# Set-up fills off GpSimd, a new order of the first transfers, a longer hold-back and three-operand VectorE forms in a three-layer kernel

## The chip, the core and the metric

One core of a Trainium2 chip runs the whole program. The metric is the device time of one execution in microseconds (us), taken as the median of several runs. One of the executions is recorded by the hardware profiler, and all rows below come from that one.

## The reference

Three layers follow each other, on 4 x 576 = 2304 tokens of width 512:

```python
scores = (q @ k.T) / 8                 # 8 heads of 64, each row sees the 64 positions up to itself
attn = exp(scores - max) / (sum + 1e-9)
x = attn @ v                           # (2304, 512)
x = relu(x @ w_in) ** 2 @ w_out        # 512 -> 2048 -> 512
do = x @ w_skip > 0                    # tokens that go to an expert, about half
e = argmax(x @ w_gate); p = softmax(x @ w_gate)[e]
out = x;  out[do] += p * (relu(x[do] @ w1[e]) @ w2[e])   # 8 experts, 512 -> 1024 -> 512
```

The weights w_in and w_out are handed over as 64-bit floats, and products are made in split precision: a value is a rounded part and a remainder, and three products stand for one.

## The kernel before

**Chunks and units.** The 18 token tiles of 128 form nine chunks of two. A unit (c, j) of the dense layer is one eighth of its hidden width for one chunk: `l1` makes 24 products of 256 columns, ScalarE squares the result and rounds it to `gh`, VectorE makes the remainder `gl` (line 491), and `l2` makes 24 products of 512 columns into two accumulators, one for each token tile. `l2` runs two units behind `l1`. The pool `gp` keeps `gh` and `gl` in three buffers.

**The first stage.** Before the units run, ten steps (`for s in range(10)`) issue the attention of tiles 0 to 3 in eight groups of four heads: scores and a mask on TensorE (`at_qk`), a maximum (L288), a scaling of it by 1/8 (L291), four exponentials on ScalarE (L302), the sum's guard and reciprocal (L306, L308), the division (L309), a transpose (`at_tr`, L317 and L319) and the product with v (`at_pv`, L335, L343, L344). Between them weights are converted from 64-bit floats (`conv_next`): ScalarE scales the high words (L220), GpSimd clips them (L221), VectorE builds the 32-bit value in three instructions (L223, L225, L227), ScalarE rounds it (L233), GpSimd makes the remainder (L234). All the loads lie on SyncE's queue, in the order in which they are issued.

**Set-up.** `setup_masks` builds the attention masks on GpSimd; `setup_routing`, called after step 4, fills the constants of the routing with GpSimd memsets and writes a table of 144 KB to memory. When tile t has its scores, `load_next` fetches q and k of the next tile with the same buffer. From tile 6 on q is padded with zeros: `load_qk(6)` first clears the buffer with two GpSimd memsets (L160, L161).

**The scheduler.** Outside of blocks marked `manual_schedule` a list scheduler orders each engine's instructions by its own estimate of time, with the program's order as priority; inside of them TensorE keeps the written order.

**The end of the dense layer.** Of the last chunk the `l2` of the last `TAIL` = 3 units is held back: first tile 0 of each (so that its routing may start), then tile 1 of each, as cover for the routing of tile 0.

**The experts.** Each expert has one block of 128 tokens that always runs (`static`) and more that run if there are that many (`extras`). `ex_x` transposes the gathered tokens on TensorE; ScalarE rounds the transposed tokens, VectorE takes the remainder (`ex_split`), and 24 products with w1 follow (`l1e`, L831). Gathers and scatters are indirect transfers from GpSimd's queue. Their descriptors live in a scratch of 8192 bytes per partition.

Of the kernel before, what the change touches and what calls it, by code (L numbers as in the profile page):

```python
# [8 lines left out]
F32 = mybir.dt.float32  # L9
F32R = mybir.dt.float32r  # L10
# [4 lines left out]
ALU = mybir.AluOpType  # L15
# [4 lines left out]
P = 128  # L20
# [15 lines left out]
HOMES = (1, 2, 0, 1, 2, 1)  # L36
# [11 lines left out]
DOT00 = 6  # L48
ROW = NE * NT
FILLS = ((2, 3), (1, 2), (1, 0), (2, 3), (2, 0), (0, 5))  # L50
TAIL = 3
FE = 1024
KF = FE // P
WIN = 64
FAR = 1 << 20
# [7 lines left out]
def body(ctx, tc, qt_d, kt_d, vw_d, wi_d, wo_d, w9_d, w9r_d, w1_d, w2_d, out):  # L63
    nc = tc.nc
# [9 lines left out]
    small = pool("small", 4)  # L74
    xtp = pool("xtp", 2)
    rp = pool("rp", 2)
    gp = pool("gp", 3)
    dram = pool("dram", 1, space=DRAM)
    ps_h = pool("ps_h", 2, space=PSUM)
    ps_acc = pool("ps_acc", 1, space=PSUM)  # L80
# [11 lines left out]
    def psa():  # L92
        turn[0] += 1
        return ps_a[turn[0] // 2 % len(ps_a)].tile([P, 512], F32, tag="a", name="a")

    def sm():
        return sp.tile([P, 512], F32, tag="sm", name="sm")
# [35 lines left out]
            out=mask.rearrange("p a b -> p (a b)"), in_=maskb.rearrange("p a b -> p (a b)"))  # L133

    def setup_routing():
        nc.gpsimd.memset(ones, 1.0)
        nc.gpsimd.memset(tri, 1.0)
        nc.gpsimd.affine_select(
            out=tri, in_=tri, pattern=[[1, P]], compare_op=ALU.is_gt,
            fill=0.0, base=0, channel_multiplier=-1)  # L140
        nc.gpsimd.iota(io8i, pattern=[[1, NE]], base=0, channel_multiplier=0)
        nc.gpsimd.tensor_copy(out=io8, in_=io8i)
        nc.gpsimd.iota(route[:, :, 0], pattern=[[P, NT]], base=0, channel_multiplier=1)
        nc.gpsimd.memset(ohsum[:, 0, :], 0.0)
        fill = sm().bitcast(I32)
        nc.gpsimd.memset(fill, FAR)
        nc.scalar.dma_start(
            out=tab_v.rearrange("p r c -> p (r c)"), in_=fill[:, 0:2 * ROW])
        nc.scalar.dma_start(out=w9, in_=w9_d)
# [6 lines left out]
    def load_qk(t):  # L156
        i = home(t)
        k_ = kvs[i > 0].tile([P, NPAIR, P + WIN], F32, tag=f"k{i}", name="k")
        if t == len(HOMES):
            nc.gpsimd.memset(qpad[0:64, :, 1, :], 0.0)  # L160
            nc.gpsimd.memset(qpad[64:128, :, 0, :], 0.0)  # L161
        if t < len(HOMES):
            nc.sync.dma_start(
                out=q_s[i], in_=qt_d[t].rearrange("h d a b -> (h d) a b"))
        else:
            for h in range(2):
                nc.sync.dma_start(out=qpad[64 * h:64 * h + 64, :, h, :], in_=qt_d[t, h])
        nc.sync.dma_start(out=k_, in_=kt_d[t])
        kt_t[t] = k_

    def load_v(t):
        i = home(t)
        v_ = kvs[i > 0].tile([P, 2, DM], F32, tag=f"v{i}", name="v")
        nc.sync.dma_start(out=v_, in_=vw_d[t])
        vw_t[t] = v_

    def load_next(t, load):
        later = [n for n in range(t + 1, NT) if home(n) == home(t)]
        if later:
            load(later[0])  # L180
# [75 lines left out]
    def at_qk(t, g):  # L256
        s = bank("qk", t, g)
        i, k_ = home(t), kt_t[t]
        early = t // CT in EARLY
        if early:  # L260
            nc.tensor.matmul(
                s.rearrange("p (a b) -> p a b", a=2), lhsT=identb,
                rhs=mask_of(t, maskb).unsqueeze(1).to_broadcast([P, 2, 2 * P]),
                start=True, stop=False, skip_group_check=True)
        for pi in range(2):
            for blk in range(2):
                u = 2 * pi + blk
                pr = 2 * g + pi
                cols = slice(u * P, (u + 1) * P)
                if t >= len(HOMES):  # L270
                    nc.tensor.matmul(
                        s[:, cols], lhsT=qpad[:, 2 * pr + blk].rearrange("p a b -> p (a b)"),
                        rhs=k_[:, pr, 64 * blk:64 * blk + P],
                        start=not early, stop=True, skip_group_check=early)
                    continue
                for h in range(2):
                    half = slice(64 * h, 64 * h + 64)
                    nc.tensor.matmul(
                        s[half, cols], lhsT=q_s[i][half, 2 * pr + blk],
                        rhs=k_[half, pr, 64 * blk:64 * blk + P],  # L280
                        start=not early, stop=True, skip_group_check=early)
        if g == 1:
            load_next(t, load_qk)
        ef = sm()
        e = ef.rearrange("p (a b) -> p a b", a=4)
        nmx = small.tile([P, 4], F32, tag="nmx", name="nmx")
        if early:
            nc.vector.tensor_reduce(  # L288
                out=nmx, in_=s.rearrange("p (a b) -> p a b", a=4), axis=AX.X, op=ALU.max,
                negate=True)  # L290
            nc.vector.tensor_scalar(  # L291
                out=nmx, in0=nmx, scalar1=1.0 / 8.0, scalar2=None, op0=ALU.mult)
        else:
            mk = mask_of(t, mask)
            for u in range(4):
                nc.vector.tensor_tensor_reduce(  # L296
                    out=e[:, u, :], in0=s[:, u * P:(u + 1) * P],
                    in1=mk[:, u % 2 * P:(u % 2 + 1) * P], scale=-1.0 / 8.0, scalar=HUGE,
                    op0=ALU.add, op1=ALU.min, accum_out=nmx[:, u:u + 1])
        sums = small.tile([P, 4], F32, tag="sum", name="sum")  # L300
        for u in range(4):
            nc.scalar.activation(  # L302
                out=e[:, u, :], in_=s[:, u * P:(u + 1) * P] if early else e[:, u, :],
                func=AF.Exp, bias=nmx[:, u:u + 1],
                scale=1.0 / 8.0 if early else -1.0, accum_out=sums[:, u:u + 1])
        nc.vector.tensor_scalar(  # L306
            out=sums, in0=sums, scalar1=1e-9, scalar2=None, op0=ALU.add)
        nc.vector.reciprocal(out=sums, in_=sums)  # L308
        nc.vector.tensor_tensor(  # L309
            out=e, in0=e, in1=sums.unsqueeze(2).to_broadcast([P, 4, P]), op=ALU.mult)  # L310
        p_t[t, g] = e

    def at_tr(t, g):
# [154 lines left out]
    def l1(c, j):  # L468
        early = bool(raw_q)
        hp = h_early[0] if early else ps_h.tile([P, 512], F32, tag="h", name="h")  # L470
        hp = hp.rearrange("p (a b) -> p a b", a=2)
        r = rp.tile([P, 512], F32, tag="r", name="r")
        xt = xt_t[c]
        for f in range(2):
            for k in range(KD):
                o = (k % 2) * 256 + f * P
                mm3(hp[:, f, :], wi_t[j, k // 2][:, 0, o:o + P], wi_t[j, k // 2][:, 1, o:o + P],
                    xt[:, 0, k, :], xt[:, 1, k, :], k == 0, k == KD - 1)
            if early:
                nc.scalar.activation(  # L480
                    out=r[:, f * CTOK:(f + 1) * CTOK], in_=hp[:, f, :], func=AF.Relu)
        if not early:
            nc.scalar.activation(  # L483
                out=r, in_=hp.rearrange("p a b -> p (a b)"), func=AF.Relu)
        gh = gp.tile([P, 2, CTOK], F32R, tag="gh", name="gh")
        gl = gp.tile([P, 2, CTOK], F32R, tag="gl", name="gl")
        ghf = gh.rearrange("p a b -> p (a b)")
        glf = gl.rearrange("p a b -> p (a b)")
        nc.scalar.activation(out=r, in_=r, func=AF.Square)  # L489
        nc.scalar.copy(out=ghf, in_=r)  # L490
        nc.vector.tensor_tensor(out=glf, in0=r, in1=ghf.bitcast(F32), op=ALU.subtract)  # L491
        g_t[c, j] = (gh, gl)

    def l2(c, j, tiles=range(CT), parts=range(2)):
# [104 lines left out]
    if True:  # L599
# [8 lines left out]
        load_qk(0)  # L608
        conv_load()
        load_qk(1)  # L610
        load_v(0)
        conv_load()
        load_qk(2)
        load_v(1)
        conv_load()
        load_v(2)
        conv_load()
        for _ in range(LOOK - 4):
            conv_load()
        setup_masks()  # L620
        acc_pool[1] = ps_s
        qk, tr, pv = grp_ops(0)
        qk1, tr1, pv1 = grp_ops(1)
# [3 lines left out]
        for s in range(10):  # L627
            if s < 8:
                qk[s]()
            if 1 <= s < 9:  # L630
                tr[s - 1]()
            if 2 <= s:
                pv[s - 2]()
            for _ in range(PRO[s]):
                conv_next()
            if s == 4:
                setup_routing()

        def w_free(kind, j):
            slot_q.extend((wp, w_tag[kind, j, h]) for h in range(2))  # L640
# [172 lines left out]

        def ex_x(tx, inner=True):
            xg = tx[2]
            pp = psa()
            for k in range(KD):
                nc.tensor.transpose(pp[:, k * P:(k + 1) * P], xg[:, k * P:(k + 1) * P], ident)
            return ex_split(pp, inner)

        def ex_block(e, tx, xt, fill=lambda i: None, nxt=lambda: None, late=False):
            ti, gw, xg, _ = tx
# [176 lines left out]
```

## Time and profile before

| what | before |
|---|---|
| median of 3 runs (lowest, highest) | 686.37 us (684.65, 687.01) |
| the profiled execution | 685.27 us, of which its span is 683.6 us |
| mean granted TensorE clock | 0.989 |
| busy TensorE, VectorE, ScalarE, GpSimd | 656.6, 415.3, 357.5, 155.4 us |

The page gives each engine's busy time, the span in 40 slices and the costliest groups. A view by windows gives the busy time of each engine in chosen stretches. The timeline gives instructions in order of time: start and duration in us, engine, line, operation, tiles written and read, count, and in brackets the idle time of the engine before it with what ended it. The profiled execution lies 1.1 us under the median.

### The profile page before, as it was taken

The page shows a single profiled execution, that of the slowest core. Times are in us where ns is not written, and L with a number is a line of the kernel's source. Part 1 is how long each engine was busy: PE and PEld are TensorE (multiplying, and loading weights), DVE is VectorE, ACT ScalarE, POOL GpSimd, SP SyncE. Part 2 cuts the span into 40 slices and gives each one's busy share as a digit, 9 for nine tenths or more (in the row PEclk, how much of TensorE's full clock was granted, in tenths as well). Part 3 has the DMA queues.
Part 4 walks back from the last instruction along what each step waited for, and adds up shares of the span by engine and source line. Part 5 has one row for each costly group of instructions (what it writes and reads, how often), then busy time and mean ns, then how long its engine had stood idle before and what let it go on. Part 6 is the DMA issues. An engine that isn't in the chain of part 4 may idle for free. (4 is left out here: it accounts for less than half of the span.)

```text
span 683.6 us, 12514 instructions
## 1 busy us (share of the span) xinstructions
PE 656.6 (96%) x4569; PEld 566.7 (83%) x4569; DVE 415.3 (61%) x1200; ACT 357.5 (52%) x821; POOL 155.4 (23%) x185
## 2 busy tenths in 40 slices
PE   7799999999999999999999999999999999999995
PEld 4588888989899889898989989899988777777774
DVE  4999977449627727716725824942735644288981
ACT  4887756544535444635535444544641544277761
POOL 5557666100100100000000000030001513044641
PEclk9899999999999999999999999999999999999998
DMA  8965453053203203203112121206592347559500
GB/s 332 349 206 172 147 168 111 1 203 98 70 32 102 70 32 101 70 32 102 40 61 85 48 71 50 83 26 230 177 317 100 111 151 279 224 161 337 222 12 8
DMA packets 45605, 88.72 MB, mean 130 GB/s; under 512 B 17806, under 2 KB 18062, under 8 KB 45392
## 3 DMA queue, kind: packets, MB, share of 16 engines
q1 hardware_dynamic: 42112, 83.38, 35.6%
q0 software_dynamic: 2976, 3.95, 1.8%
q8 instruction: 47, 0.77, 0.5%
q10 hardware_dynamic: 432, 0.32, 0.2%
q14 instruction: 38, 0.31, 0.1%
HBM read 79.07 MB, written 12.49 MB: 134 GB/s over the span
## 5 line engine op out<-in xcount | busy, mean ns | idle before, releaser
L464 PE MATMUL h<-xt,wi 128*128 128x256 f32 x576 | 165.3, 287 | 2.1 <-ACT r L480 2.1
L465 PE MATMUL h<-xt,wi 128*128 128x256 f32 x576 | 165.6, 287 | 0.3 <-DVE xt L344 0.3
L466 PE MATMUL h<-xt,wi 128*128 128x256 f32 x576 | 164.0, 285 | 0.0
L464 PE MATMUL acc<-wo,gh 128*128 128x512 f32 x288 | 116.3, 406 | 1.1 <-ACT gh L490 1.0
L464 PEld LDWEIGHTS h<-xt,wi 128*128 128x128 f32 x576 | 110.6, 192 | 6.4 <-ACT r L480 3.1
L465 PEld LDWEIGHTS h<-xt,wi 128*128 128x128 f32 x576 | 110.6, 192 | 3.4 <-DVE xt L344 0.6
L465 PE MATMUL acc<-wo,gh 128*128 128x512 f32 x288 | 112.6, 393 | 0.0
L466 PE MATMUL acc<-wo,gl 128*128 128x512 f32 x288 | 112.0, 393 | 0.0
L491 DVE TENSOR_TENSOR gl<-r,gh 128x512 fp32r<-128x512 f32 x72 | 52.4, 728 | 96.5 <-ACT gh L490 95.0
L466 PEld LDWEIGHTS h<-xt,wi 128*128 128x128 f32 x576 | 110.7, 192 | 0.0
L456 POOL DMA_INDIRECT tab_d<-route,posi x18 | 19.5, 1084 | 362.6 <-DVE posi L447 263.7
L483 ACT ACTIVATE r<-h 128x512 f32<-128x512 f32 x58 | 34.5, 595 | 98.4 <-PE h L466 94.7
L375 DVE CUSTOM_DVE_ANT_0 prod<-sm,w9b 128x512 f32<-128x512 f32 x108 | 74.0, 685 | 1.9 <-ACT sm L352 1.5
L466 PEld LDWEIGHTS acc<-wo,gl 128*128 128x128 f32 x288 | 54.1, 188 | 12.6 <-DVE gl L491 0.8
L464 PEld LDWEIGHTS acc<-wo,gh 128*128 128x128 f32 x288 | 54.1, 189 | 11.1 <-ACT gh L490 2.1
L465 PEld LDWEIGHTS acc<-wo,gh 128*128 128x128 f32 x288 | 54.3, 189 | 8.6 <-issue 0.2
L548 DVE TENSOR_TENSOR e_s<-e_s,e_s 128x1024 fp32r<-128x1024 f32 x34 | 42.1, 1258 | 11.9 <-ACT e_s L546 11.5
L302 ACT ACTIVATE sm<-sm,nmx 128x128 f32<-128x128 f32 x96 | 37.5, 392 | 20.7 <-DVE nmx L296 20.3
L319 ACT COPY sm<-a 128x512 f32<-128x512 f32 x36 | 21.4, 594 | 48.8 <-PE a L317 48.8
L489 ACT ACTIVATE r<-r 128x512 f32<-128x512 f32 x72 | 45.6, 634 | 1.5
L490 ACT CAST gh<-r 128x512 fp32r<-128x512 f32 x72 | 44.6, 619 | 1.5
L546 ACT CAST e_s<-e_s 128x1024 fp32r<-128x1024 f32 x42 | 42.9, 1050 | 2.5 <-PE acc L466 2.0
(205 smaller groups left out, 1144.6 us busy)
## 6 DMA issues: line engine op xcount, KB each, us to landing
e_s<-in_w_dram SPq DMA_DIRECT2D x54, 512.0 KB, 6.4
v<-in_vw_dram SPq DMA_DIRECT2D x18, 512.0 KB, 3.4
ri<-in_wi_dram SPq DMA_DIRECT2D x16, 512.0 KB, 4.1
ro<-in_wo_dram SPq DMA_DIRECT2D x16, 512.0 KB, 3.7
k<-in_kt_dram SPq DMA_DIRECT2D x18, 384.0 KB, 4.2
e_r<-in_w_dram SPq DMA_DIRECT2D x10, 512.0 KB, 6.6
x_d<-sm SPq DMA_DIRECT2D x17, 256.0 KB, 2.5
out_dram<-sm SPq DMA_DIRECT2D x17, 256.0 KB, 3.1
```

Of the source, the lines that this page charges most:

```text
L302: nc.scalar.activation(out=e[:, u, :], in_=s[:, u * P:(u + 1) * P] if early else e[:, u, :], func=AF.Exp, bias=nmx[:, u:u + 1], scale=1.0 ...
L319: nc.scalar.copy(out=pt, in_=pp)
L375: nc.vector.tensor_tensor_reduce(out=prod, in0=x2_t[t], in1=w9b_t[0][:, j, :], scale=1.0, scalar=0.0, op0=ALU.mult, op1=ALU.add, accum_out ...
L464: nc.tensor.matmul(out_ap, lhsT=ah, rhs=bh, start=start, stop=False)
L465: nc.tensor.matmul(out_ap, lhsT=ah, rhs=bl, start=False, stop=False)
L466: nc.tensor.matmul(out_ap, lhsT=al, rhs=bh, start=False, stop=stop)
L483: nc.scalar.activation(out=r, in_=hp.rearrange("p a b -> p (a b)"), func=AF.Relu)
L489: nc.scalar.activation(out=r, in_=r, func=AF.Square)
L490: nc.scalar.copy(out=ghf, in_=r)
L491: nc.vector.tensor_tensor(out=glf, in0=r, in1=ghf.bitcast(F32), op=ALU.subtract)
L546: nc.scalar.copy(out=hi, in_=raw)
L548: eng.tensor_tensor(out=lo, in0=raw, in1=hi.bitcast(F32), op=ALU.subtract)
```

## The change

It does seven things. The memsets of `setup_routing` go to VectorE, and the call moves up to just behind `setup_masks`. The first loads get another order: each weight load but the first and last comes one load of v earlier. q and k of tile 6 are loaded after the scores of tile 5 instead of those of tile 2, with the two memsets that precede them. Four VectorE instructions (L291, L306, L309, L491) are written in the form that has two tensors and a scalar; two of them get a tile of zeros as second tensor. `TAIL` becomes 4 and `gp` gets a fourth buffer. For the blocks of `extras`, `ex_x` works in two halves in two PSUM banks. The scratch of the indirect transfers is halved.

```diff
-TAIL = 3
+TAIL = 4
-    gp = pool("gp", 3)
+    gp = pool("gp", 4)
     def setup_routing():
-        nc.gpsimd.memset(ones, 1.0)
-        nc.gpsimd.memset(tri, 1.0)
+        nc.vector.memset(ones, 1.0)
+        nc.vector.memset(tri, 1.0)
...
-        nc.gpsimd.memset(ohsum[:, 0, :], 0.0)
+        nc.vector.memset(ohsum[:, 0, :], 0.0)
         fill = sm().bitcast(I32)
-        nc.gpsimd.memset(fill, FAR)
+        nc.vector.memset(fill, FAR)
...
-        if g == 1:
+        if g == 1 and t != 2:
             load_next(t, load_qk)
+        if g == 1 and t == len(HOMES) - 1:
+            load_next(2, load_qk)
...
-            nc.vector.tensor_scalar(
-                out=nmx, in0=nmx, scalar1=1.0 / 8.0, scalar2=None, op0=ALU.mult)
+            nc.vector.scalar_tensor_tensor(
+                out=nmx, in0=nmx, scalar=1.0 / 8.0, in1=tiny.to_broadcast([P, 4]),
+                op0=ALU.mult, op1=ALU.add)
...
-        nc.vector.tensor_scalar(
-            out=sums, in0=sums, scalar1=1e-9, scalar2=None, op0=ALU.add)
+        nc.vector.scalar_tensor_tensor(
+            out=sums, in0=sums, scalar=1e-9, in1=tiny.to_broadcast([P, 4]),
+            op0=ALU.add, op1=ALU.add)
         nc.vector.reciprocal(out=sums, in_=sums)
-        nc.vector.tensor_tensor(
-            out=e, in0=e, in1=sums.unsqueeze(2).to_broadcast([P, 4, P]), op=ALU.mult)
+        nc.vector.scalar_tensor_tensor(
+            out=e, in0=e, scalar=1.0, in1=sums.unsqueeze(2).to_broadcast([P, 4, P]),
+            op0=ALU.mult, op1=ALU.mult)
...
-        nc.vector.tensor_tensor(out=glf, in0=r, in1=ghf.bitcast(F32), op=ALU.subtract)
+        nc.vector.scalar_tensor_tensor(
+            out=glf, in0=r, scalar=1.0, in1=ghf.bitcast(F32), op0=ALU.mult, op1=ALU.subtract)
...
         load_qk(1)
+        conv_load()
         load_v(0)
+        load_qk(2)
         conv_load()
-        load_qk(2)
         load_v(1)
         conv_load()
         load_v(2)
-        conv_load()
         for _ in range(LOOK - 4):
             conv_load()
         setup_masks()
+        setup_routing()
...
-            if s == 4:
-                setup_routing()
...
+        def ex_x_halves(xg):
+            hi = gp.tile([P, 512], F32R, tag="gh", name="xh2")
+            lo = gp.tile([P, 512], F32R, tag="gl", name="xl2")
+            pps = [psa(), psa()]
+            cut = [slice(n * 256, (n + 1) * 256) for n in range(2)]
+            for n in range(2):
+                for k in range(2):
+                    nc.tensor.transpose(
+                        pps[n][:, k * P:(k + 1) * P],
+                        xg[:, (2 * n + k) * P:(2 * n + k + 1) * P], ident)
+                nc.scalar.copy(out=hi[:, cut[n]], in_=pps[n][:, 0:256])
+            for n in range(2):
+                nc.vector.tensor_tensor(
+                    out=lo[:, cut[n]], in0=pps[n][:, 0:256], in1=hi[:, cut[n]].bitcast(F32),
+                    op=ALU.subtract)
+            return hi, lo
...
-                   dynamic_dma_scratch_size=8192)
+                   dynamic_dma_scratch_size=4096)
```

## Rows read from the trace of the kernel before

**Rows 1.** The page, its first part: TensorE's busy time, share, instructions.

```profile
PE 656.6 (96%) x4569; PEld 566.7 (83%) x4569; DVE 415.3 (61%) x1200; ACT 357.5 (52%) x821; POOL 155.4 (23%) x185
```

**Rows 2.** By windows: us, PE, PEld, DVE, ACT, POOL busy; clock, DMA share, GB/s.

```profile
24.00:28.00 4.00, 2.70 (x49) 2.13 (x50) 3.97 (x5) 3.06 (x14) 3.16 (x6) 1.00 1.12 284
...
32.00:36.00 4.00, 3.73 (x28) 3.35 (x27) 4.00 (x11) 2.89 (x11) 1.77 (x3) 0.50 0.91 295
```

**Rows 3.** Timeline of ScalarE, first stage: the first three weight scalings.

```profile
7.18 0.67 ACT L220 ACTIVATE ri<-ri 128x512 f32<-128x512 f32 x1 [4.44 <-DMA ri<-in_wi_dram]
...
11.32 0.69 ACT L220 ACTIVATE ri<-ri 128x512 f32<-128x512 f32 x1 [0.94 <-DMA ri<-in_wi_dram]
...
15.53 0.68 ACT L220 ACTIVATE ri<-ri 128x512 f32<-128x512 f32 x1 [1.63 <-DMA ri<-in_wi_dram]
```

**Rows 4.** Timelines of VectorE, GpSimd, ScalarE and TensorE from 24 to 31 us.

```profile
24.34 2.90 DVE L291 TENSOR_SCALAR nmx<-nmx 128x4 f32<-128x4 f32 x1
...
24.32 0.52 POOL L160 MEMSET qpad<- 64x512 f32 x1
24.81 1.27 POOL L234 TENSOR_TENSOR wi<-f,wi 128x512 fp32r<-128x512 f32 x1
...
26.06 0.52 POOL L146 MEMSET sm<- 128x512 int32 x1
26.56 0.66 POOL L221 TENSOR_SCALAR ro<-ro 128x512 f32<-128x512 f32 x1
...
27.34 0.37 ACT L302 ACTIVATE sm<-s,nmx 128x128 f32<-128x128 f32 x1 [0.94 <-DVE nmx L291]
...
28.89 0.38 PE L261 MATMUL s<-maskb,identb 128*128 128x512 bf16 x1 [1.47 <-ACT sm L302]
...
30.71 1.11 PE L317 MATMUL a<-ident,sm 128*128 128x128 f32 x4 [0.43 <-DVE sm L309]
```

**Rows 5.** Timeline of TensorE: one product of `l1` at either clock.

```profile
33.33 0.41 PE L466 MATMUL h<-xt,wi 128*128 128x256 f32 x1
...
38.08 0.28 PE L465 MATMUL h<-xt,wi 128*128 128x256 f32 x1
```

**Rows 6.** By line (durations min/median/max in ns); timelines of GpSimd and VectorE.

```profile
L291 DVE TENSOR_SCALAR nmx<-nmx x12: 155/417/2899, 8.6 to 76.5; 128x4 f32<-128x4 f32 x12
...
L309 DVE TENSOR_TENSOR sm<-sm,sum x36: 676/690/1798, 11.9 to 450.6; 128x512 f32<-128x512 f32 x36
...
59.76 1.30 POOL L234 TENSOR_TENSOR wi<-f,wi 128x512 fp32r<-128x512 f32 x1 [1.59 <-ACT wi L233]
...
60.39 1.21 DVE L309 TENSOR_TENSOR sm<-sm,sum 128x512 f32<-128x512 f32 x1
```

**Rows 7.** By line: the padded scores, with their first and last start.

```profile
L271 PE MATMUL a<-k,qpad x192: 270/275/275, 140.2 to 446.6; 128*128 128x128 f32 x192
```

**Rows 8.** Timelines of ScalarE and TensorE at the end of the dense layer.

```profile
510.46 1.04 ACT L546 CAST e_s<-e_s 128x1024 fp32r<-128x1024 f32 x1
...
513.01 0.62 ACT L490 CAST gh<-r 128x512 fp32r<-128x512 f32 x1
...
513.68 0.50 PE L464 MATMUL acc<-wo,gh 128*128 128x512 f32 x1 [1.00 <-ACT gh L490]
```

**Rows 9.** TensorE's waits (total, times, longest); timelines of an extra block; a half cast.

```profile
PE h L831 <- ACT xh L729: 2.2, 3, 0.7
...
570.10 0.63 PE L818 MATMUL a<-ident,sm 128*128 128x128 f32 x4 [0.95 <-DVEq L900]
570.81 0.59 ACT L729 CAST xh<-a 128x512 fp32r<-128x512 f32 x1 [2.65 <-PE a L818]
...
28.72 0.38 ACT L343 CAST xt<-xp 128x256 fp32r<-128x256 f32 x1
```

**Rows 10.** Indirect gathers: duration by line; issues with median us to landing.

```profile
L705 POOL DMA_INDIRECT xg<-x_d,tabs x15: 1012/1293/2043, 534.9 to 647.3; - x15
...
xg<-x_d,tabs POOLq DMA_INDIRECT x15, 3.5
```

More of the change, by code (lines that the diff above doesn't have):

```diff
@@ L815, in ex_x @@
             xg = tx[2]
+            if inner:
+                return ex_x_halves(xg)
             pp = psa()
```

## The prediction

> **What bounds the kernel now.** The first part of the page comes first: TensorE is busy for 96% of the span [rows 1], so only time in which it waits, or in which its clock is low, can be won. The view by windows says where that is. Two stretches of the first stage stand out [rows 2]: from 24 to 28 us TensorE is busy for 2.70 of 4.00 us while VectorE is full with five instructions, and from 32 to 36 us TensorE is nearly full, but its granted clock is 0.50. From the end of that stage to the end of the dense layer TensorE runs without gaps worth naming, so whatever the first stage gives back is kept until the end. The reader then looks at TensorE's waits and the timelines around them: a wait of 1.00 us at the end of the dense layer [rows 8] and three waits of some 0.7 us in front of extra blocks [rows 9]. The other engines matter only where they end one of these.
>
> **The order of the first transfers.** ScalarE waits for the second and third weight loads, 0.94 and 1.63 us [rows 3], and its queue is in order, so the exponentials behind them wait too. The landings that released the first and the second scaling lie 4.14 us apart, and between them the queue carried 1664 KB (v of tile 0, one weight load, q and k), so 512 KB take 1.27 us. In the new order the second and third weight loads lie 512 KB further ahead: the first wait goes, the second shrinks by 1.27. Against that, the table of 144 KB that `setup_routing` writes now goes out at the start, 0.36 us at the same rate. v comes 1.27 us later; its first use lies after all of this. I take 1.0 us; the ends are 0.3 (other work of ScalarE fills the time) and 1.3.
>
> **The stall of VectorE.** L291 scales a tile of 4 columns, and at 24.34 it takes 2.90 us [rows 4]. All that time GpSimd runs without a gap: the clearing of the padded q (L160), a remainder (L234), the fill of the table (L146) and a clip (L221), and L291 ends as the last one does. The change takes the memsets out of the place: the fill goes to VectorE, at the start, where VectorE has nothing to do, and the clearing goes behind tile 5. The price on TensorE's path is not 2.75 us, though: ScalarE had other work and waited for 0.94, then TensorE for 1.47 before the next scores and 0.43 before the next transpose [rows 4]. Without the stall the scores start 0.94 us earlier and the transpose another 0.4: I take 1.4 us. The ends are 0.9 and 2.7, the whole of it, since VectorE is full until 36 us and all its later work comes earlier.
>
> **The clock.** After that low stretch the granted clock is 0.50 from 32 to 36 us [rows 2], the lower of the two levels, and a product of `l1` takes 0.41 us against 0.28 [rows 5]. At the same pace these 4 us hold 2 us of work, and with their edges some 3 us could be won at full clock. If TensorE waits less before, the clock need not fall. But then TensorE catches up with VectorE, which is full in that stretch. I take 1.5 us; the ends are 0 and 3.
>
> **The three-operand forms.** What they do where GpSimd is at work is in no row. For the two large ones the nearest row is the form they replace: L309 at 60.39 has both inputs in SBUF and takes 1.21 us instead of 0.68 at the least; it ends 0.54 us after L234, which started before it [rows 6]. I take it that the new form, with the same two inputs, waits likewise: nothing gained, nothing lost; at most what all the small stalls hold. L291 has a median of 0.42 us against 0.16 at the least [rows 6], so its twelve lose some 0.26 us each beside the long one, 3 us in all up to 77 us, of which I count a third in the first stage: an end of 1 us. The Trainium skill speaks here against part of the change (SBUF — State Buffer, section "Who interferes with whom"): a `tensor_scalar` in its two-port mode is blocked by any GpSimd instruction, while an instruction with two SBUF inputs is blocked by one that reads SBUF. By that rule L309 and L491 gain nothing and L291 is freed from memsets alone; the trace agrees on the two old forms (1.21 us beside L234, 2.90 us across memsets too). If the new form were free of GpSimd, the sum would be about 1 us larger.
>
> **Tile 6.** Its q and k are loaded later, with two memsets of 0.52 us (1.04 us of GpSimd, which waits for ScalarE most of the time), and SyncE's queue holds the weight loads behind them for as long, which are five ahead. By the code they are issued at least three units before their first use at 140.2 us [rows 7]. Nothing.
>
> **The hold-back.** At 513.68 TensorE has waited 1.00 us for `gh` of the last unit [rows 8]: ScalarE put casts of expert weights (L546) of 1.04 us each, two of them, ahead of its own steps. With `TAIL` = 4 the last `l1` comes half a unit earlier, and tile 0 of one more unit stands in front of the product that waits: six products of 512 columns more between the two, over 1 us even by the 0.28 us of one of 256 columns [rows 5]. The wait goes, 1.0 us; the wait for `gl` behind it may give 0.15. The second of those casts then goes into a buffer that is freed only by the held-back unit, so it can't stand in front any more. The loads of two w2 parts of expert 2 move behind the routing of the last tile, and are used only in expert 1's block. Ends 0 (ScalarE finds other work to put in front) and 1.2. Work is moved, not added.
>
> **The halves.** In front of an extra block TensorE makes four transposes (0.63 us), ScalarE casts 512 columns (0.59), and the first product waits for 0.7 [rows 9]. With halves the cast starts after two transposes, 0.3 us earlier, and takes 0.38, the row of a cast of 256 columns, so the first product comes 0.3 + 0.2 = 0.5 us earlier; the second cast is ready before the third product asks for it. There are three such waits; at the first ScalarE is still with the cast before, so only 0.2 there. Together 1.2, less some for two more instructions per block: I take 1.0, with ends 0.4 and 1.3.
>
> **The sum.** 1.0 + 1.4 + 1.5 + 1.0 + 1.0 = 5.9 us. The profiled execution took 685.27 us and would take 679.4; it lies 1.1 us under the median, and against the median it is 686.37 - 5.9 = 680.5 us. A fourth buffer of `gp` costs nothing but room; the halved scratch is costed at nothing, with a rival of its own.
>
> **The rivals.** (a) The clock falls again in the first stage, in the same place or another. For it: the clock also depends on gaps that stay. It takes back the 1.5: 682.0 us. (b) The first stage refills: ScalarE and VectorE are close to full there, the scheduler orders them anew, and the change hardly does there what it says. Then the first stage gives 1.0 of its 3.9 us: 683.4. (c) The new form isn't held up by GpSimd at all, and VectorE, the engine that is full in the first stage, gets the small stalls back too, with the whole 2.7 of the long one and the clock: 3 us more, about 677.5. Against it stands the row of the old form with two inputs. (d) Slower: the halved scratch holds too few descriptors, and indirect transfers go one by one. Their place is GpSimd's queue in the expert stage. Now they follow each other in 1.29 us and land in 3.5 [rows 10], so up to three are under way at once; with one at a time an expert's two gathers and up to two scatters take 14 us, as long as an expert has now (fifteen gathers in 112 us, two an expert). With GpSimd's other work its queue would set the pace: an estimated 1 to 1.5 us more for each of six experts, 6 to 9, and 2 x 2.2 for the second gather behind the first two in front of the first extra block, so 10 to 13 us more and some 692 us. It decides only if half the scratch holds less than two transfers, and three under way at full size speak against that.
>
> **How the numbers follow.** The forecast as summed has 0.53, (a) 0.20, (b) 0.12, (c) 0.10, (d) 0.05. The likeliest case alone spans 678.5 to 682. The range for eight in ten leaves out (d) and the upper end of (b) on one side and half of (c) on the other: 676.5 to 684.5. A measurement of this kernel can tell 0.3%, about 2.1 us, from no change, so "same" is 684.3 to 688.4: parts of (a) and (b), 0.09. Slower is (d), 0.05. Faster is the rest, 0.86.
>
> **What would show it.** In the profile after, the second L220 should show no wait and the third a shorter one; no L291 near 2.9 us; a clock of 1.00 in the slices after 24 us; the first gapless products of `l1` about 4 us earlier, and every later landmark of the dense layer with them; no wait for `gh` in front of the last unit's `l2`; waits near 0.2 us in front of extra blocks. The prediction is wrong if TensorE's first stage ends less than 2 us earlier, if a new wait stands in the held-back part, or if the indirect transfers follow each other in their landing time.

## The result, and the profile after

The changed kernel is slower: median 690.23 us of 12 runs (687.98 to 691.40), the kernel before beside it 685.49 of 12 (682.50 to 687.51), ratio 1.0066 with a 95% interval of 1.0050 to 1.0083. The forecast was 680.5, with a range from 676.5 to 684.5.

Where the time lies is read from two landmarks of TensorE and from the end of the program. Between its first and its last padded score the dense layer takes the same time in both kernels (306.4 us before, 306.5 after), so the start of the last one tells what the first stage has cost. By line, after (count, durations min/median/max in ns, first and last start): that row, answering to [rows 7], and the first products with the experts' w1.

```profile
L271 PE MATMUL a<-k,qpad x192: 270/275/275, 148.5 to 455.0; 128*128 128x128 f32 x192
...
L855 PE MATMUL h<-e_xt,xh x36: 387/431/501, 536.3 to 661.4; 128*128 128x512 f32 x36
```

The second of them before, which does not stand ahead:

```profile
L831 PE MATMUL h<-e_xt,xh x36: 387/395/501, 529.5 to 655.8; 128*128 128x512 f32 x36
```

The last row of GpSimd's timeline (start, duration), before and then after:

```profile
677.73 0.97 POOL L880 DMA_INDIRECT out_dram<-xg,tabs  x1 [10.05 <-DVE xg L878]
```
```profile
683.32 0.97 POOL L904 DMA_INDIRECT out_dram<-xg,tabs  x1 [9.84 <-DVE xg L902]
```

The first stage lost 8.4 us (455.0 against 446.6). At the first expert product the kernel is 6.8 behind, so the end of the dense layer gave back 1.6; at the last indirect transfer it is 5.6 behind, so the experts gave back another 1.2. The spans differ by 4.0 (687.6 and 683.6), so 1.6 more came after that last transfer, where nothing was forecast. The medians of twelve runs differ by 4.7. All the loss is in the first stage, where a gain of 3.9 had been forecast.

Now that stage. By windows (us, PE, PEld, DVE, ACT, POOL busy; clock, DMA share, GB/s), after:

```profile
8.00:12.00 4.00, 1.20 (x17) 0.94 (x17) 2.81 (x6) 1.41 (x7) 1.24 (x2) 1.00 1.03 416
16.00:20.00 4.00, 2.27 (x16) 1.46 (x12) 4.00 (x9) 0.93 (x2) 1.26 (x3) 0.84 1.03 403
...
40.00:44.00 4.00, 1.96 (x20) 1.66 (x20) 3.95 (x10) 3.67 (x15) 3.41 (x6) 0.65 0.84 290
44.00:48.00 4.00, 4.00 (x32) 3.57 (x28) 3.89 (x9) 2.83 (x8) 2.59 (x4) 0.50 0.70 247
```

TensorE is busy for 1.20, 2.27 and 1.96 of 4 us in three of them, and runs at the lower clock in the fourth. Two of the holes are also holes of ScalarE: it is busy for 1.41 us from 8 to 12 and for 0.93 from 16 to 20. Its timeline, then one row of VectorE's, and then TensorE's, name what they stood at:

```profile
7.40 0.67 ACT L220 ACTIVATE ri<-ri 128x512 f32<-128x512 f32 x1 [4.67 <-DMA ri<-in_wi_dram]
10.66 0.68 ACT L220 ACTIVATE ri<-ri 128x512 f32<-128x512 f32 x1 [2.59 <-DMA ri<-in_wi_dram]
11.23 0.35 ACT L305 ACTIVATE sm<-s,nmx 128x128 f32<-128x128 f32 x1
...
14.89 0.67 ACT L220 ACTIVATE ri<-ri 128x512 f32<-128x512 f32 x1 [0.27 <-DMA ri<-in_wi_dram]
19.07 0.62 ACT L233 CAST wi<-f 128x512 fp32r<-128x512 f32 x1 [3.51 <-DVE nmx L293]
```
```profile
18.30 0.68 DVE L227 SCALAR_TENSOR_TENSOR f<-ri,h 128x512 int32<-128x512 int32 x1
```
```profile
12.77 0.38 PE L261 MATMUL s<-maskb,identb 128*128 128x512 bf16 x1 [3.57 <-ACT sm L305]
...
20.78 1.12 PE L340 MATMUL xp<-sm,v 128*64 128x64 f32 x16 [1.69 <-ACT sm L324]
...
42.04 1.09 PE L322 MATMUL a<-ident,sm 128*128 128x128 f32 x4 [3.25 <-DVE sm L313]
```

The second weight scaling, L220, found its data earlier than before (10.66 us against 11.32 [rows 3]), though by 0.66 us and not by 1.27. But it now stands ahead of the first group's exponentials: ScalarE waits 2.59 us at it, the exponentials start at 11.23, and TensorE waits 3.57 for them. A second time a conversion stands in front: from 15.5 to 19.07 ScalarE waits at the rounding L233 for VectorE's part of that conversion, and the copy and the exponentials behind it wait too. (By the code the rounding reads `f`, which VectorE's L227 writes until 18.98; the row names L293, which ended just after it, at 19.05.) The third hole is at the division L313, on a VectorE that is busy for 3.95 of these 4 us. So the theory was that the list scheduler made another order for these in-order queues out of the new loads, and that this order is the loss; the rival was that another part of the change, or the transfers themselves, held up the stage.

### The profile page after: what moved, and what is told of

It is laid out like the page before. It is cut to its first block, busy times and chain, and to the rows that moved or that the text cites. A ratio compares the mean times of both kernels' runs of the same rounds, so it can differ in the third digit from the quotient of the medians.

```text
span 687.6 us, 12519 instructions
## 1 busy us (share of the span) xinstructions
PE 658.8 (96%) x4569; PEld 567.8 (83%) x4569; DVE 413.3 (60%) x1207; ACT 356.8 (52%) x824; POOL 150.2 (22%) x181
## 3 DMA queue, kind: packets, MB, share of 16 engines
q0 software_dynamic: 2976, 3.95, 1.9%
## 5 line engine op out<-in xcount | busy, mean ns | idle before, releaser
L496 DVE SCALAR_TENSOR_TENSOR gl<-r,gh 128x512 fp32r<-128x512 f32 x72 | 50.7, 706 | 108.1 <-ACT gh L495 103.0
L554 DVE TENSOR_TENSOR e_s<-e_s,e_s 128x1024 fp32r<-128x1024 f32 x35 | 44.1, 1276 | 11.8 <-ACT e_s L552 11.2
L495 ACT CAST gh<-r 128x512 fp32r<-128x512 f32 x72 | 44.5, 620 | 1.6
```

Source lines behind the costliest of these rows:

```text
L496: nc.vector.scalar_tensor_tensor(out=glf, in0=r, scalar=1.0, in1=ghf.bitcast(F32), op0=ALU.mult, op1=ALU.subtract)
L554: eng.tensor_tensor(out=lo, in0=raw, in1=hi.bitcast(F32), op=ALU.subtract)
```

## The experiments

**One part undone, one part alone.** `no_loads` is the changed kernel with the old order of the first transfers; `only_loads` is the kernel before with the new one; `late` is the kernel before with what works at the end (`TAIL`, `gp`, scratch, halves).

`no_loads`, against the changed kernel (`only_loads` is the reverse, against the kernel before):

```diff
         load_qk(1)
-        conv_load()
         load_v(0)
+        conv_load()
         load_qk(2)
-        conv_load()
         load_v(1)
         conv_load()
         load_v(2)
+        conv_load()
```

> The changed kernel with the first transfers in the order of the kernel before; all the rest of the change stays. Theory 1 (order of ScalarE's queue): the new load order made the list scheduler put the second weight scaling, L220, ahead of the first group's exponentials, where it waits for its landing; with the old load order ScalarE's order is the old one, TensorE reaches l1 after its first gap at least 5 us earlier than in the changed kernel, and the time is 680 to 683 us. Theory 2 (another part holds up the first stage: the fills and table write at the front, the three-operand forms beside GpSimd, the memsets of tile 6): the loss of some 8 us stays, 688 to 691 us.

> The kernel before with the new order of the first transfers alone. Theory 1: the second weight scaling stands ahead of the first exponentials, TensorE's gap in front of its first masks grows from 1.3 to some 3.6 us, and the kernel is slower by as much as the changed kernel's first stage was, 7 to 8 us: 691 to 694 us. Theory 2: the load order itself gains what was forecast or does nothing, 684 to 686 us.

> The kernel before with the late parts alone: four units held back, a fourth buffer of gp, the halves in front of extra blocks and the halved scratch. From the two traces, the lead of the kernel before shrinks by 1.6 us at the end of the dense layer and by 1.2 in the experts: 2.8 us faster, 682 to 683.5 us, by both theories. If the gain at the end of the dense layer came only because the changed kernel was late in the first stage (its loads of weights had more time), 1.2 us alone: 684.3.

Measured: `no_loads` 677.41 us (ratio to the kernel before 0.9886, 0.9863 to 0.9908), `only_loads` 694.07 (1.0134, 1.0107 to 1.0161), `late` 679.13 (0.9918, 0.9896 to 0.9940). So the new order of the loads costs 9.0 us alone and 12.8 within the change, and without it the change gains 7.6; `no_loads` lies below the 680 to 683 expected. `late` gained 5.9 where 2.8 was expected; the single parts below account for most of it. Timelines: the second scaling and TensorE's second masks in `only_loads`, then ScalarE in `no_loads`:

```profile
11.43 0.65 ACT L220 ACTIVATE ri<-ri 128x512 f32<-128x512 f32 x1 [2.23 <-DMA ri<-in_wi_dram]
...
13.52 0.59 PE L261 MATMUL s<-maskb,identb 128*128 128x512 bf16 x1 [4.57 <-ACT sm L302]
```
```profile
8.62 0.37 ACT L305 ACTIVATE sm<-s,nmx 128x128 f32<-128x128 f32 x1 [0.85 <-DVE nmx L293]
...
11.69 0.66 ACT L220 ACTIVATE ri<-ri 128x512 f32<-128x512 f32 x1 [1.56 <-DMA ri<-in_wi_dram]
```

With the old loads the exponentials go first, at 8.62, and the scaling waits behind them. Other parts of the change are thereby out as the cause. This still leaves two causes together: the transfers themselves, and the order that comes with them.

**Order and transfers taken apart.** `pinned` keeps the new loads and ties the scalings of the second to fourth conversion, and the roundings of the second and third, behind the exponentials that they follow in the kernel before. `fullpin` keeps the new loads and ties the first 170 or so instructions each of ScalarE and VectorE, each behind the one that precedes it in `no_loads`; in its trace both engines have the order of `no_loads` throughout the first 95 us. `forced` is the opposite: the kernel before, with its old loads, and both engines tied in the order of `only_loads` (the first two scalings are written ahead of the steps, so that they can go first). A tie can name only an instruction that the program writes earlier, so the order of `forced` is that of `only_loads` on ScalarE up to 40 us, while on VectorE some neighbours change places from 17 us on.

`pinned` (`PIN_C` gives each conversion its group), and then `fullpin` and `forced`, where each call looks up its place in a written list:

```diff
-        nc.scalar.activation(out=hf, in_=hf, func=AF.Copy, scale=F64_SCALE)
+        with behind(PIN_C.get(m)):
+            nc.scalar.activation(out=hf, in_=hf, func=AF.Copy, scale=F64_SCALE)
...
-        nc.scalar.activation(out=hf, in_=hf, func=AF.Copy, scale=F64_SCALE)
+        p_scalar.activation(out=hf, in_=hf, func=AF.Copy, scale=F64_SCALE)
...
+            while p > 0 and self.order[p - 1] not in self.ins:
+                p -= 1
+                with self.tc.issue_after(self.ins[self.order[p - 1]].ins):
+                    r = f(*a, **kw)
```

> The changed kernel whole, new load order too, but with the weight scalings and roundings of the second to fourth conversion tied by hand behind the exponentials that they follow in the kernel before. Theory 1: with ScalarE's old order the new loads do no harm, and the second scaling finds its data (landed at 10.7 us); 679 to 683 us. Theory 2: the order of ScalarE isn't the cause, 688 to 691 us. If the loads themselves came too late (v of tile 0, k and q of tile 2), the time lies between, about 685.

> The changed kernel whole, with the new order of the first transfers, but on ScalarE and VectorE the first 160 instructions each are tied, one behind the other, in the order that they have with the old transfers. Only the order of the transfers differs from that kernel (677.4 us). Theory 1: the harm lies in the order that the scheduler makes for these two engines; with the old order the new transfers cost nothing and give 0 to 1.3 us: 676 to 678 us. Theory 2: the harm lies in the transfers themselves (v, q or k come too late, or a weight load holds up SyncE's queue); the time stays at 684 us or more, as where only four conversions were tied (685.1).

> The kernel before with its own order of the first transfers, but ScalarE and VectorE tied in the order that the scheduler makes for the new transfers (second weight scaling ahead of the first exponentials). The fourth cell of the square: old or new transfers by old or new order of the two engines. Theory 1 (the order does the harm): as slow as the kernel with the new transfers alone (694.1 us) or slower, since the second scaling now waits for a landing at 11.3 instead of 10.7 us: 693 to 696. Theory 2 (only the new transfers together with that order do harm): 685 to 688.

Measured: `fullpin` 677.09 us (0.9877, 0.9855 to 0.9898), `forced` 698.71 (1.0171, 1.0148 to 1.0194), `pinned` 685.07 (0.9998, 0.9985 to 1.0012). This makes a square:

| | order made for the old loads, on ScalarE and VectorE | order made for the new loads |
|---|---|---|
| old loads | `no_loads` 677.4; before 685.0 | `forced` 698.7 |
| new loads | `fullpin` 677.1 | changed kernel 690.2; `only_loads` 694.1 |

`no_loads`, `fullpin` and the changed kernel have the other parts of the change; before, `forced` and `only_loads` don't. Along a row the order changes: 13.1 us (690.2 - 677.1) with the new loads, and 13.4 (698.7 - 685.3, the kernel before in the runs beside it) with the old ones. Down a column the loads change: -0.3 in the old order, which can't be told from nothing, and -4.6 in the new one (`only_loads` against `forced`, whose orders are not quite the same). The harm is in the order; the new loads in an unchanged order do none. `forced` came out above its 693 to 696, `fullpin` in its 676 to 678. `pinned` missed its 679 to 683 and fell where late loads were the explanation; `fullpin`, with the same loads, rules that out. Why the scheduler makes that order was not tried. Timelines of ScalarE and TensorE in `forced`, then of ScalarE in `fullpin` (L29 is the helper's line in both):

```profile
12.39 0.65 ACT L29 ACTIVATE ri<-ri 128x512 f32<-128x512 f32 x1 [3.78 <-DMA ri<-in_wi_dram]
12.95 0.35 ACT L29 ACTIVATE sm<-s,nmx 128x128 f32<-128x128 f32 x1
...
14.48 0.59 PE L351 MATMUL s<-maskb,identb 128*128 128x512 bf16 x1 [5.54 <-ACT sm L29]
```
```profile
8.65 0.65 ACT L29 ACTIVATE ri<-ri 128x512 f32<-128x512 f32 x1 [5.91 <-DMA ri<-in_wi_dram]
9.21 0.35 ACT L29 ACTIVATE sm<-s,nmx 128x128 f32<-128x128 f32 x1
...
11.63 0.68 ACT L29 ACTIVATE ri<-ri 128x512 f32<-128x512 f32 x1 [0.93 <-DMA ri<-in_wi_dram]
...
15.84 0.68 ACT L29 ACTIVATE ri<-ri 128x512 f32<-128x512 f32 x1 [1.64 <-DMA ri<-in_wi_dram]
```

In `fullpin` the new loads ought to have shown the gain that the prediction counted: the second scaling without a wait, the third with less. It shows 0.93 and 1.64, against 0.94 and 1.63 [rows 3]. The first one started 1.47 us later in that execution (8.65 against 7.18), as it waited for its data until then. The fourteen traces, one execution each, show where the gain stays out. From the first landing to the second it takes 2.89 to 3.28 us in the five with the new loads and 4.14 to 4.59 in the nine with the old, shorter by about what was computed. But with the new loads the first landing comes at 7.40 to 8.65, with the old at 6.85 to 7.29 in seven traces and at 7.94 and 8.47 in two. Why it comes later was not tried.

`pinned` got the front right and lost time later. Its VectorE leaves the order of `no_loads` at 18.2 us and its ScalarE at 21.8; the next conversions move ahead. TensorE waits 2.54 us at 35.27 for a division (L323). After its products have ended at 36.56, it waits 2.37 for the step L495 between `l1` and `l2`, and ScalarE runs a scaling, a rounding and a cast without a gap in front of that step. Timelines of ScalarE and TensorE:

```profile
37.13 0.70 ACT L228 ACTIVATE ro<-ro 128x512 f32<-128x512 f32 x1
37.67 0.66 ACT L242 CAST wo<-f 128x512 fp32r<-128x512 f32 x1
38.18 0.42 ACT L358 CAST xt<-xp 128x256 fp32r<-128x256 f32 x1
38.45 0.44 ACT L495 ACTIVATE r<-h 128x256 f32<-128x256 f32 x1
...
35.27 0.63 PE L332 MATMUL a<-ident,sm 128*128 128x128 f32 x4 [2.54 <-DVE sm L323]
...
38.94 0.58 PE L479 MATMUL h<-xt,wi 128*128 128x256 f32 x1 [2.37 <-ACT r L495]
```

**How much of it is the first place.** `swap1` is the changed kernel with only its second weight load moved ahead of v of tile 0; the later two stay where they were in the kernel before.

```diff
         load_v(0)
         load_qk(2)
-        conv_load()
         load_v(1)
         conv_load()
         load_v(2)
+        conv_load()
```

> The changed kernel with the first weight load alone moved: the second weight load ahead of v of tile 0, the two later ones where they were. In this program the second scaling stands ahead of the first exponentials as in the changed kernel, the third and fourth don't move ahead. Theory 1, if the first place is what costs: TensorE's gap before its second masks is 3.6 us as in the changed kernel, and nearly all of the loss is there, 686 to 690 us. If each conversion that moves ahead adds its own loss (the kernel with four conversions tied still lost 8 us against the fully tied one, with no first gap), this one loses only the first gap's 2.3 us and what the clock adds: 679 to 683.

Measured: 687.17 us (1.0026, 1.0015 to 1.0037), 9.8 above `no_loads`. TensorE's gap is 4.52 us, and ScalarE's second scaling waits 2.24 (timelines):

```profile
11.19 0.65 ACT L220 ACTIVATE ri<-ri 128x512 f32<-128x512 f32 x1 [2.24 <-DMA ri<-in_wi_dram]
...
13.29 0.59 PE L261 MATMUL s<-maskb,identb 128*128 128x512 bf16 x1 [4.52 <-ACT sm L305]
```

So the second load in first place, with all that the scheduler then makes of the rest, costs 9.8 us; the new loads with the front tied cost 8.0 (`pinned` against `fullpin`); and the new loads with nothing tied cost 13. Theory 1's size for the first place holds, though TensorE's gap was 4.52 and not 3.6 us, but it isn't the only costly one. The two don't add up: in both, the order of what follows is another than in `no_loads` as well.

**The front parts without the loads.** `only_stt` has only the four three-operand forms, which leaves the order of work on ScalarE, VectorE and GpSimd as it is (the traces agree over the first 95 us); `only_routing` has only the fills on VectorE and the earlier call, which makes another order on ScalarE from 32 us on.

`only_stt` (one of four), and then `only_routing` (one fill of four, and the call):

```diff
-            nc.vector.tensor_scalar(
-                out=nmx, in0=nmx, scalar1=1.0 / 8.0, scalar2=None, op0=ALU.mult)
+            nc.vector.scalar_tensor_tensor(
+                out=nmx, in0=nmx, scalar=1.0 / 8.0, in1=tiny.to_broadcast([P, 4]),
+                op0=ALU.mult, op1=ALU.add)
...
-        nc.gpsimd.memset(fill, FAR)
+        nc.vector.memset(fill, FAR)
...
         setup_masks()
+        setup_routing()
```

> The kernel before with the four three-operand forms alone; the order of all engines stays as it is. L291 at 24.3 us has one memset and two GpSimd instructions that read SBUF beside it. If the new form waits only for those that read SBUF, the 2.90 us become at most 1.8 (behind L234) or some 1 and the first stage gains 0.5 to 1.4 us: 683.6 to 684.5. If it waits as before, 685.0.

> The kernel before with the routing's fills on VectorE and its call moved ahead of the steps, nothing else. Forecast of the prediction: with the memset of 0.52 us out of the way, and the table's transfer and the fills early, the stall of L291 ends at least 0.5 us earlier; 0.9 to 2.7 us, with up to 1.5 of the clock: 681 to 684. If the stall stays behind L234 and the memsets of tile 6, and the table's 144 KB delay the first weight loads by 0.36, 685.0 to 685.5.

Measured: 682.29 us (0.9954, 0.9937 to 0.9972) and 682.34 (0.9958, 0.9940 to 0.9975): either gains 3.0 us. For `only_stt` 683.6 to 684.5 was expected, so it gained more than that. The place of the 2.90 us stall [rows 4] in the timelines of VectorE and GpSimd, first of `only_stt`, then of `only_routing`, and last of `no_loads`, which has both edits:

```profile
23.46 0.52 POOL L160 MEMSET qpad<- 64x512 f32 x1
23.48 0.14 DVE L291 SCALAR_TENSOR_TENSOR nmx<-nmx,tiny 128x4 f32<-128x4 f32 x1
...
23.95 1.27 POOL L234 TENSOR_TENSOR wi<-f,wi 128x512 fp32r<-128x512 f32 x1
```
```profile
24.42 1.27 POOL L234 TENSOR_TENSOR wi<-f,wi 128x512 fp32r<-128x512 f32 x1
24.53 1.22 DVE L291 TENSOR_SCALAR nmx<-nmx 128x4 f32<-128x4 f32 x1
```
```profile
23.99 1.26 POOL L234 TENSOR_TENSOR wi<-f,wi 128x512 fp32r<-128x512 f32 x1
24.09 1.19 DVE L293 SCALAR_TENSOR_TENSOR nmx<-nmx,tiny 128x4 f32<-128x4 f32 x1
```

In the new form the instruction takes 0.14 us beside a memset; the old one, with one fill less in GpSimd's queue, takes 1.22, until the remainder L234 ends. With both edits it again starts just behind L234 and takes 1.19, so there the form gives nothing. Either edit takes the long stall away, so the gains must not be added: on top of `late`, the fills, the forms and the part of tile 6 together give 1.7 us by the medians (679.13 - 677.41) and 3.6 by the landmark of one execution each (446.4 and 442.8).

**The late parts one by one.** `scratch` only halves the scratch; `only_tail` has `TAIL` = 4 and the fourth buffer, and the halved scratch, without which the buffer finds no room; `only_halves` has the halves with the scratch as before.

`scratch`; `only_tail` beside that line; `only_halves` (its function is the one of the change):

```diff
-                   dynamic_dma_scratch_size=8192)
+                   dynamic_dma_scratch_size=4096)
...
-TAIL = 3
+TAIL = 4
-    gp = pool("gp", 3)
+    gp = pool("gp", 4)
...
+            if inner:
+                return ex_x_halves(xg)
```

> The kernel before with the scratch of the indirect transfers halved, nothing else. In all traces with the halved scratch 5.35 us lie between the last product and the end, in the two without it 6.90. Theory A: the scratch sets what follows the last transfer: 1.55 us less there, 683.5 us. Theory B: it is the other late work: 685.0. The rival of the prediction (gathers one at a time) would give 695.

> The kernel before with TAIL = 4 and the fourth buffer of gp, which needs the room of the halved scratch, so that is in too. Forecast of the prediction for the hold-back: 1.0 us; by the trace of the kernel with all late parts 1.6, and up to 2.5 in the last experts' static blocks if these come from the hold-back and not from the halves, and 1.55 at the end if theory A on the scratch holds: 680 to 682.5 us; without these two 683.5.

> The kernel before with the halves in front of extra blocks alone, the scratch as before. Forecast of the prediction: 1.0 us, 684.0 us. If the 2.5 us that the kernel with all late parts gains in the last static blocks come from the halves (a changed order of ScalarE there), 681.5.

Measured: `scratch` 683.56 us (0.9968, 0.9949 to 0.9987), `only_tail` 681.97 (0.9956, 0.9939 to 0.9973), `only_halves` 682.71 (0.9972, 0.9958 to 0.9986). `scratch`, the page's first line and GpSimd's last row:

```profile
span 682.3 us, 12514 instructions
```
```profile
678.00 0.97 POOL L880 DMA_INDIRECT out_dram<-xg,tabs  x1 [9.83 <-DVE xg L878]
```

By line, the two landmarks of `only_tail`:

```profile
L271 PE MATMUL a<-k,qpad x192: 270/275/276, 139.3 to 445.7; 128*128 128x128 f32 x192
...
L831 PE MATMUL h<-e_xt,xh x36: 387/470/628, 527.0 to 654.5; 128*128 128x512 f32 x36
```

TensorE's waits in front of extra blocks (total, times, longest) in `only_halves`, then in the changed kernel:

```profile
PE h L850 <- ACT xh L833: 1.1, 3, 0.5
```
```profile
PE h L855 <- ACT xh L838: 1.0, 3, 0.5
```

`scratch` ends 3.3 us after the end of its last transfer's issue (682.3 - 678.97), the kernel before 4.9 (683.6 - 678.70): 1.6 less, and the median moves by 1.5. All eight traces with the halved scratch have 3.3 us there, all six with the full one 4.8 to 4.9. `only_tail` has 81.3 us between the two landmarks against 82.9 before: 1.6 from the hold-back, which with the scratch makes the 3.1 measured. It is 81.2 to 81.3 in all seven traces with `TAIL` = 4, 82.8 to 82.9 in all seven with 3. `only_halves` has 1.1 us of waits where there were 2.2 [rows 9]. Its median gained 2.3. From the first to the last of the 36 products in the second landmark's row it takes 124.2 us against 126.3 before, but `scratch`, without the halves, takes 125.1, so what the halves give beyond the 1.1 stays open.

## Why the prediction was wrong

**The order of the first transfers** is the step that failed. It counted 1.0 us of gain, with ends of 0.3 and 1.3, all positive. The sum took ScalarE's queue to stay as it was, and the waits to shrink in place. In the changed kernel the second and third data did come 0.66 and 0.64 us earlier, but the program put the earlier loads' scalings ahead of the exponentials, and the step measures a loss of 12.8 us within the change. A smaller error lies beside it: the sum held the first landing fixed, and in the traces with the new loads it comes later; in an unchanged queue the loads give 0.3 us, less than can be told, and not 1.0. Rival (b) named this mechanism, the scheduler ordering anew, but priced it as a gain that is kept to 1.0 of 3.9; it had to have an end below nothing. The slower rival was looked for in the scratch instead. That queue's order stood in the rows: a scaling of 0.7 us that waits for its load, with exponentials behind it that TensorE needs [rows 3, 4]. One load moved ahead of one other was enough to change places (`swap1`).

**The stall of VectorE and the clock** were forecast at 2.9 us together, and under the old loads the fills alone gave 3.0; on top of `late`, the fills, the forms and the part of tile 6 gave 1.7. The fill did leave that place, and the stall fell from 2.90 to 1.22 us; but `only_routing` also has another order on ScalarE from 32 us on, so how much of its 3.0 us the stall is was not told apart. The clearing did not move behind tile 5: its memsets start at 28.96 and 29.53 us in the changed kernel, and at 22.29 and 22.87 in `no_loads`. In the changed kernel little of the gain is seen, for its order has no such stall: the longest L291 of `only_loads`, in the old form, is 0.99 us.

```profile
L291 DVE TENSOR_SCALAR nmx<-nmx x12: 159/288/994, 8.4 to 85.1; 128x4 f32<-128x4 f32 x12
```

It fits that the other parts together are worth 7.6 us under the old loads (685.03 - 677.41) and 3.8 under the new ones (694.07 - 690.23), and that the landmark lies at 455.8 us without them and at 455.0 with them. The low clock came back in other places, 40 to 48 us above all, as rival (a) said. How much the clock itself is worth can't be told: `scratch`, `only_tail`, `only_halves` and `late` have the first stage of the kernel before, instruction by instruction, and their landmark lies at 448.1, 445.7, 445.5 and 446.4, so one execution differs by up to 2.6 us from another there. The latest and the earliest go with the first weight load, which lands at 8.47 us in `scratch` and at 6.85 in `only_halves`.

**The three-operand forms.** "Nothing" was wrong: alone they are worth 3.0 us. Rival (c) took them to be free of GpSimd altogether; they are half free. Beside memsets they run at full speed, which is what takes the long stall away. Beside instructions that read SBUF they wait as the old ones did, as the 1.19 us of `no_loads` above show. Timelines of GpSimd and VectorE, after:

```profile
14.70 1.27 POOL L234 TENSOR_TENSOR wi<-f,wi 128x512 fp32r<-128x512 f32 x1 [2.64 <-ACT wi L233]
14.85 1.67 DVE L313 SCALAR_TENSOR_TENSOR sm<-sm,sum 128x512 f32<-128x512 f32 x1
...
28.96 0.52 POOL L161 MEMSET qpad<- 64x512 f32 x1
29.36 0.16 DVE L309 SCALAR_TENSOR_TENSOR sum<-sum,tiny 128x4 f32<-128x4 f32 x1
```

The division beside L234 takes 1.67 us and ends 0.55 us after it. The old form's 1.21 us ended 0.54 after its L234 [rows 6]; it only started later in it. So the large form waits as before, as forecast. The guard of the sum, beside a memset, takes 0.16. The rule that the prediction took from the Trainium skill (SBUF — State Buffer, section "Who interferes with whom") holds in both: two SBUF inputs contend with a GpSimd instruction that reads SBUF, not with one that only writes it. The prediction cited it, and yet costed the small forms at nothing.

**Tile 6** was costed at nothing. No run has that part alone. Built alone it leaves every engine's instructions in the order of the kernel before, so that it costs nothing follows from the program and is not measured.

**The hold-back and the halves** were right in mechanism: forecast 1.0 each, measured 1.6 by the landmarks, above its end of 1.2, and 1.1 by the waits. TensorE's wait for `gh` at the end of the dense layer is gone from its waits in the changed kernel, and the three in front of extra blocks total 1.0 us, the longest 0.5, as forecast.

**The scratch** was costed at nothing and is worth 1.5 us. The rival that put a loss of 10 to 13 us there fell.

With the load order left out, the prediction's sum is 4.9 us; the kernel without it gained 7.6. That the two lie no further apart is partly luck, for the terms missed in both directions: the late parts gained 5.9 where the sum had 2.0 (the scratch's 1.5 and the hold-back's 0.6 are most of what is known of that), and the front parts added 1.7 where it had 2.9.

`fullpin` (677.09 us) and `no_loads` (677.41) beat both kernels; the second does it with no ties, by leaving the transfers in their old order.

## What to carry to other kernels

Where a scheduler orders the queues, an edit to loads is also an edit to the order of every in-order engine that waits for them; before costing it, name for each such engine the instruction that waits for the moved load and what stands behind it, and give the step an end below nothing of the size of that wait. Test it by undoing the load order alone and by holding the queues' order fixed; one place too early in a queue can cost far more than the wait it shows (9.8 us here, where the gap on TensorE was 4.5), since the scheduler places the later work anew as well. Two edits that take away the same stall count once.

## What the runs showed of the hardware

After the last indirect transfer's issue the program ends 1.6 us sooner with a scratch of 4096 bytes per partition than with one of 8192 (3.3 against 4.9 us); why was not tried. A VectorE instruction with two SBUF inputs of 128 x 4 took 0.14 us beside GpSimd's memset, where the one-input form with a scalar had taken 2.90 across memsets and others [rows 4]; beside GpSimd's remainder, which reads SBUF, the two-input form took 1.19.
